# y transposed back through fewer PSUM banks, two expert halves summed in PSUM, nine early products of zeros, and an instruction order drawn from 42 candidates

## The chip, the core and the metric

The kernel runs on one core of one Trainium2 chip. The metric is the device time of one execution in microseconds. Five engines work side by side, each through its own list of instructions in a fixed order: TensorE (PE, with its weight loads shown as PEld), VectorE (DVE), ScalarE (ACT), GpSimd (POOL) and SyncE (SP), which issues the DMAs. They wait for each other by semaphores only.

## What is computed

Attention with a top-32 mask per row, then a mixture of four experts weighted per token, then a gated product with a last projection. All in fp32.

```python
# attention: B, H, S, D = 2, 8, 576, 64
scores = scale * np.matmul(q, k.transpose(0, 1, 3, 2))
kth = np.partition(scores, -top_k, axis=-1)[..., -top_k:-top_k + 1]   # top_k = 32
scores = np.where(scores >= kth, scores, -1e9)
attn = softmax(scores); x = attn @ v
# experts: N, D, E, F = 1152, 512, 4, 1024
for e in range(E):
    out += p[:, e:e + 1] * (np.maximum(x @ w1[e], 0.0) @ w2[e])
# gated: d_ff = 1536
return ((x @ w_a) * (x @ w_b)) @ w_out
```

## The kernel before

The 1152 tokens are nine tiles of 128 (eight regular ones and one that mixes the last 64 rows of both batches). They are cut into four groups of 1, 2, 3 and 3 tiles. Attention runs over groups, head pairs (four) and tiles, 36 steps in all; each step has two heads. For each head PE makes scores of 128 x 576 (`scores`, matmuls of 288 columns), ACT copies them to SBUF (L618), DVE finds the 32 largest by four MAX8 (L638) with three MATCH_REPLACE8 between them (L646), ACT and POOL mask and exponentiate (L669, L673, L677, L688), PE transposes the weights and multiplies by v. The result of one head pair goes to `xf` (group 0) or `xs` (the others) as the input of the experts.

The experts of group 0 (`plain`) run in fp32 straight from the loaded weights. Those of groups 1 to 3 (`experts`) split every operand into a high part (a rounded copy made by ACT, L804) and a low part (a subtraction on POOL or, for the last group, on DVE, L805), and multiply three times. `first` makes one 128-row piece of x @ w1 in a bank of PSUM; ACT and DVE empty it into a high and a low part (L875, L879). `second` multiplies four such pieces (half of F) by w2, 12 matmuls of 512 columns into one bank; DVE then scales the bank by the expert's share and adds it to y in SBUF (L897; the very first time it only scales, L895). So each expert has two halves and each half of each tile one such addition.

When a group's y is complete, `replace` transposes it back to columns: for each of four blocks of 128 columns it takes one PSUM bank, makes one transpose per tile of the group, and ACT (L917) and DVE (L921) empty the bank into the high and low halves of `xs`. The call is deferred (`pending`): it is issued behind the first weight unit of the next group, or in `gated`, ahead of its third block of columns. `gated` is the last stage and runs over all nine tiles. Its own weights are unpacked by ACT and DVE beforehand (`d_unit`).

PSUM has eight banks of 512 fp32 columns. Three of them form the pool `m` (`ms`), from which `first`, `second`, `plain`, `gated` and `replace` all take their banks in the order in which they were asked for; two pairs (`att`) and one bank (`o`) belong to attention.

The order of the instructions is not written by hand: every helper adds an operation with an assumed duration, a key and what it waits for, and `Plan.order` runs through time as a list scheduler, per engine taking the ready operation with the smallest key whose buffers are free. What it gives is the order in which the program is emitted; on the chip each engine then follows its list.

Of the kernel before, what the change touches and what calls it, by code (L numbers as in the profile page):

```python
# [2 lines left out]

# [31 lines left out]
class Slots:  # L35
# [13 lines left out]

    def settle(self):  # L50
        self.queue.sort(key=lambda t: t.need)
        for i, t in enumerate(self.queue):
            t.n = i

# [14 lines left out]
class Op:  # L69
    __slots__ = ("engine", "hold", "lag", "key", "emit", "waits", "after", "tiles", "n", "start", "left", "at", "nbytes", "port", "since")  # L70
# [6 lines left out]

class Plan:
    def __init__(self):
        self.ops = []  # L80

    def add(self, engine, hold, emit, key, after=(), tiles=(), lag=100, nbytes=0, port=False):
        op = Op()
        op.engine, op.hold, op.lag, op.key, op.emit = engine, hold, lag, key, emit
        op.waits = list({id(a): a for a in after if a is not None}.values())
        op.tiles = list({id(t): t for t in tiles}.values())
        op.after, op.n, op.start, op.nbytes, op.port, op.since = [], len(self.ops), None, nbytes, port, 0.0
        for t in op.tiles:
            t.users += 1
        self.ops.append(op)  # L90
        return op

    def order(self):
        for op in self.ops:
            op.left, op.at = len(op.waits), op.since
            for w in op.waits:
                w.after.append(op)
# [69 lines left out]
        while len(done) < len(self.ops):  # L167
            moved = False
            for engine in free:
# [73 lines left out]
LATE = 2  # L243
SLACK = 1200
# [4 lines left out]
def body(tc, q, k, v, probs, w1, w2, wa, wb, wo, out):  # L249
    nc = tc.nc  # L250
# [97 lines left out]
    atts = Slots("att", [ps[:, 3 + 2 * i:5 + 2 * i] for i in range(2)])  # L348
    os_ = Slots("o", [ps[:, 7]])
# [486 lines left out]
    def second(hts, units, t0, after):  # L836

        p = ms.tile()
        last = None
        N = len(hts)  # L840
        for i, ((h, hd, n), (u, ud, uv, part)) in enumerate(zip(hts, units)):
            def emit(i=i, h=h, n=n, uv=uv, part=part):
# [3 lines left out]
                for m, (l, r) in enumerate(((hhi, whi), (hhi, wlo), (hlo, whi))):  # L846
                    mm(p.ap, l, r, start=(i == 0 and m == 0), stop=(i == N - 1 and m == 2))
# [7 lines left out]
    def experts(c):  # L855
# [7 lines left out]
        yd = {}  # L863
        for e in range(E):

            late = 2 if c == len(GROUPS) - 1 else c == len(GROUPS) - 2 and e >= LATE
            for f0 in range(0, F, 512):
# [22 lines left out]
                for t in range(T):  # L890
                    p, o = second(hts, units, t * 128, ())
                    i = TILES.index(tiles[t])
                    yv = lambda t=t: y.ap[:, t * DM:(t + 1) * DM]
                    if e == 0 and f0 == 0:
# [10 lines left out]
    def replace(c, y, yd):  # L905
        T = len(GROUPS[c])
        cs = columns_of(c)
        for a in range(KD):
            p = ms.tile()

            def emit(a=a, p=p):
                for t in range(T):
                    tr(p.ap[:, t * 128:(t + 1) * 128], y.ap[:, t * DM + a * 128:t * DM + (a + 1) * 128], ident)

            o = tensor(T * TURN_F, emit, 1000 + nxt(), list(yd.values()), [p, y])
# [3 lines left out]
            lo = vector(  # L919
                dve(T * 128),  # L920
                lambda a=a, p=p: nc.vector.tensor_tensor(xs[:, 1, a, cs], p.ap[:, 0:T * 128], xs[:, 0, a, cs], op=ALU.subtract),  # L921
                -1000, [hi], [p],
            )
            ydone[c, a] = [hi, lo]
# [195 lines left out]
```

## Time and profile before

| | |
|---|---|
| median of 3 runs | 850.61 us (850.32 to 910.58) |
| the profiled execution | 849.56 us, span 847.8 us |
| PE busy | 817.2 us (96%) |
| DVE busy | 715.7 us (84%) |
| ACT busy | 537.5 us (63%) |
| POOL busy | 267.5 us (32%) |
| moved by DMA | 117.06 MB |

The profile is of one execution. Busy time counts an engine's instructions; a row of the timeline is a run of like instructions with its start, its length, and in brackets how long the engine stood idle before it and for whom it waited. The granted clock of TensorE has two levels here, 1.2 and 2.4 GHz.

### The profile page before, as it was taken

Reading aid. Unit: us, or ns where it says so; the run is one execution under the profiler, and the core shown is the slowest. Engines: PE = TensorE matmul, PEld = TensorE weight load, DVE = VectorE, ACT = ScalarE, POOL = GpSimd, SP = SyncE. Lnnn points to the kernel's source line nnn. Section 1 sums busy time; section 2 is a strip of 40 time slices with the busy share of each in tenths; the row PEclk is TensorE's granted clock in tenths of the full one; section 3 lists DMA queues with packets and bytes.
Section 4 is the critical chain, followed back from the end, with each engine's and each line's share of the span. In section 5 each row is a group of like instructions: output and inputs, shape, how many; then the busy total and the mean of one; then the engine's idle time right before and its main releaser. Section 6 shows DMA issues by size and latency. Waiting matters only on the chain.

```text
span 847.8 us, 14175 instructions
## 1 busy us (share of the span) xinstructions
PE 817.2 (96%) x5168; PEld 728.4 (86%) x5168; DVE 715.7 (84%) x1387; ACT 537.5 (63%) x1034; POOL 267.5 (32%) x250
## 2 busy tenths in 40 slices
PE   6689999999999999999999999999999999999997
PEld 5467787788988888999889898899898989999996
DVE  7999999999999999999969998555435888989823
ACT  6888887998999898788665654334225535344220
POOL 3534343879897966755210000000000000000000
PEclk9999999999999999999999999999999999999999
DMA  5849877755554544333246654343001322323003
GB/s 170 287 115 310 306 241 231 230 174 173 147 191 132 156 169 151 105 101 100 78 131 193 208 177 160 124 131 118 2 1 50 100 68 82 100 83 93 26 1 111
DMA packets 83509, 117.06 MB, mean 138 GB/s; under 512 B 10608, under 2 KB 54640, under 8 KB 83440
## 3 DMA queue, kind: packets, MB, share of 16 engines
q1 hardware_dynamic: 83440, 116.17, 43.8%
q8 instruction: 40, 0.66, 0.3%
q14 instruction: 29, 0.24, 0.1%
HBM read 109.07 MB, written 7.08 MB: 137 GB/s over the span
## 4 chain that ended last, share of the span: by engine, by line
PE 78%; DVE 10%; ACT 7%; issue 2%; POOL 1%; DMA 0%; POOLq 0%; ACTq 0%; DVEq 0%
PE ps L373 72%; PE ps L376 6%; DVE low L638 3%; DVE low L646 2%; DVE mid L805 1%; ACT low L688 1%; ACT low L618 1%; ACT low L669 1%; ACT big L429 1%; ACT low L677 1%; ACT big L570 1%; DVE mid L879 1%; ACT low L743 1%; POOL big L433 1%; POOL low L673 1%
## 5 line engine op out<-in xcount | busy, mean ns | idle before, releaser
L373 PE MATMUL ps<-xs,mid 128*128 128x384 f32 (+1 forms) x1152 | 204.1, 322 | 1.3 <-DVE mid L879 1.3
L638 DVE MAX8 low<-low 128x8 f32<-128x576 f32 x288 | 203.6, 747 | 2.1 <-ACT low L618 2.0
L373 PE MATMUL ps<-mid 128*128 128x512 f32 x768 | 198.3, 395 | 0.3 <-POOL mid L805 0.3
L373 PEld LDWEIGHTS ps<-xs,mid 128*128 128x128 f32 x1152 | 186.0, 191 | 9.6 <-DVE mid L879 1.5
L373 PEld LDWEIGHTS ps<-mid 128*128 128x128 f32 x768 | 139.5, 188 | 24.0 <-DVE mid L879 0.7
L646 DVE MATCH_REPLACE8 low<-low 128x576 f32<-128x576 f32 x216 | 159.3, 744 | 0.0
L373 PE MATMUL ps<-xs,big 128*128 128x384 f32 x864 | 152.6, 335 | 0.0
L373 PEld LDWEIGHTS ps<-xs,big 128*128 128x128 f32 x864 | 150.2, 188 | 1.2 <-DVE xs L921 0.2
L804 ACT ACTIVATE mid<-raw 128x1024 fp32r<-128x1024 f32 x96 | 101.5, 1061 | 43.4 <-issue 27.2
L805 POOL TENSOR_TENSOR mid<-raw,mid 128x1024 fp32r<-128x1024 f32 x48 | 115.3, 2407 | 15.3 <-ACT mid L804 11.3
L673 POOL TENSOR_TENSOR low<-low 128x576 f32<-128x576 f32 x70 | 99.3, 1437 | 27.9 <-ACT low L669 27.8
L875 ACT ACTIVATE mid<-ps 128x384 fp32r<-128x384 f32 (+1 forms) x96 | 43.6, 455 | 51.4 <-PE ps L373 46.0
L373 PE MATMUL ps<-big,mid 128*128 128x512 f32 x324 | 76.0, 391 | 0.0
L373 PEld LDWEIGHTS ps<-big,mid 128*128 128x128 f32 x324 | 60.5, 188 | 12.5 <-DVE low L1053 0.4
L879 DVE SCALAR_TENSOR_TENSOR mid<-ps,mid 128x384 fp32r<-128x384 f32 (+1 forms) x96 | 48.4, 507 | 26.0 <-ACT mid L875 25.5
L805 DVE TENSOR_TENSOR mid<-raw,mid 128x1024 fp32r<-128x1024 f32 x48 | 58.5, 1220 | 9.6 <-ACT mid L804 8.8
L688 ACT ACTIVATE low<-low 128x576 f32<-128x576 f32 x70 | 51.4, 778 | 12.4 <-DVE low L685 12.4
L618 ACT ACTIVATE low<-ps 128x576 f32<-128x576 f32 x72 | 46.8, 650 | 18.4 <-POOL low L673 13.1
L669 ACT ACTIVATE low<-low 128x576 f32<-128x576 f32 x70 | 51.9, 778 | 9.8 <-POOL low L663 9.7
L897 DVE SCALAR_TENSOR_TENSOR ys<-ps,pr,ys 128x512 f32<-128x512 f32 x56 | 41.8, 746 | 18.9 <-PE ps L373 18.3
L1050 ACT ACTIVATE low<-ps 128x384 f32<-128x384 f32 x36 | 17.7, 491 | 62.8 <-PE ps L373 62.7
L376 PE MATMUL ps<-identr,low 128*128 128x128 f32 (+1 forms) x360 | 50.0, 279 | 5.2 <-ACT low L688 4.6
(87 smaller groups left out, 1050.9 us busy)
## 6 DMA issues: line engine op xcount, KB each, us to landing
raw<-in_moe_w_dram SPq DMA_DIRECT2D x122, 512.0 KB, 3.8
big<-kscr SPq DMA_DIRECT2D x20, 576.0 KB, 4.8
low<-in_v_dram SPq DMA_DIRECT2D x24, 256.0 KB, 3.8
low<-in_moe_w_a_dram SPq DMA_DIRECT2D x12, 512.0 KB, 4.3
low<-in_moe_w_b_dram SPq DMA_DIRECT2D x12, 512.0 KB, 3.8
low<-in_moe_w_out_dram SPq DMA_DIRECT2D x12, 512.0 KB, 3.6
kscr<-big SPq DMA_DIRECT2D x8, 576.0 KB, 4.9
ys<-in_moe_w_dram SPq DMA_DIRECT2D x6, 512.0 KB, 4.8
```

Source lines behind the costliest of these rows:

```text
L373: nc.tensor.matmul(out, l, r, **kw)
L376: nc.tensor.transpose(out, a, i)
L618: S, lambda: nc.scalar.activation(s.ap.rearrange("p (c n) -> p c n", c=2), at.ap[:, :, 0:HALF], AF.Copy),
L638: 62 + 1.04 * width, lambda at=at, cs=cs: nc.vector.max(m8v()[:, x, cs], at()), key + 0.02 * r, [done],
L646: lambda at=at, cs=cs: nc.vector.match_replace(out=src[1](), in_to_replace=m8v()[:, x, cs], in_values=at(), imm_value=LOW),
L669: S, lambda x=x, s=s: nc.scalar.activation(e[x].ap, s.ap, AF.Relu, bias=endv()[:, x, 1:2], scale=-STEEP),
L673: pool_(S), lambda x=x, s=s: nc.gpsimd.tensor_tensor(e[x].ap, s.ap, e[x].ap, op=ALU.subtract), ks, [a], [s, e[x]]
L688: S, lambda x=x: nc.scalar.activation(e[x].ap, e[x].ap, AF.Copy, scale=sums.ap[:, x:x + 1]),
L804: hi = scalar(1024, lambda: nc.scalar.activation(u.ap[:, 0:1024], r.ap, AF.Copy), 500 + s, [ld], [u, r], sbuf=True)
L805: sub = lambda eng: eng.tensor_tensor(u.ap[:, 1024:2048], r.ap, u.ap[:, 0:1024], op=ALU.subtract)
L875: n, lambda h=h, p=p: nc.scalar.activation(h.ap[:, 0:n], p.ap[:, 0:n], AF.Relu), -1000, [o], [h, p]
L879: lambda h=h, p=p: nc.vector.scalar_tensor_tensor(h.ap[:, n:2 * n], p.ap[:, 0:n], 0.0, h.ap[:, 0:n], op0=ALU.max, op1=ALU.subtract),
```

## The change

Four things change.

- `replace` packs G blocks of columns into one bank: 4 for group 0 (one tile), 2 for group 1 (two tiles), 1 for the groups of three tiles. ACT and DVE empty a bank with one instruction each. For groups 2 and 3 the banks come from a new pool `mls`, the five banks that attention used; that pool may hand out a bank only when attention's pools are done.
- For the last group, `second` keeps the sum of an expert's two halves in one bank of `mls`: the first half starts the accumulation, the second ends it, and only then DVE scales and adds (24 additions become 12).
- Before anything else PE makes nine products of 128 x 256 out of a block of zeros, which DVE writes first (`blank`).
- `Plan.best` builds 42 orders. In each, every operation is assumed to end late by a random amount of up to 25 (in the planner's ns), from a certain stage of time on; each order is replayed three times with random lateness of engines and DMAs, and the one with the smallest mean replayed end is emitted.

```diff
+ORDERS, RERUNS, SHAKE, LATE_ENGINE, LATE_DMA, LOG = 42, 3, 25.0, 40.0, 800.0, False
+    def best(self):
+        found = None
+        for r in range(ORDERS):
+            draw = random.Random(r)
+            since = STAGES[r * len(STAGES) // ORDERS]
+            for op in self.ops:
+                if r:
+                    op.late = found[3][op.n] if found[4][op.n] < since else draw.uniform(0.0, SHAKE)
+            got = self.order()
+            mean = sum(self.rerun(got, random.Random(i)) for i in range(RERUNS)) / RERUNS
+            if found is None or mean < found[0]:
+                found = mean, got, {id(t): t.slot for op in got for t in op.tiles}, [op.late for op in self.ops], [op.start for op in self.ops]
...
-                    end = now + op.hold + op.lag
+                    end = now + op.hold + op.lag + op.late
...
-    atts = Slots("att", [ps[:, 3 + 2 * i:5 + 2 * i] for i in range(2)])
-    os_ = Slots("o", [ps[:, 7]])
+    atts = Slots("att", [ps[:, 3 + 2 * i:5 + 2 * i] for i in range(2)], "psum", [(3, 5), (5, 7)])
+    os_ = Slots("o", [ps[:, 7]], "psum", [(7, 8)])
+    mls = Slots("ml", [ps[:, 3 + i] for i in range(5)], "psum", [(3 + i, 4 + i) for i in range(5)])
+    atts.rank, os_.rank, mls.rank = 0, 0, 1
...
-    def second(hts, units, t0, after):
-        p = ms.tile()
-        last = None
+    def second(hts, units, t0, after, bank=None, begin=True, end=True, last=None):
+        p = bank or ms.tile()
...
-                    mm(p.ap, l, r, start=(i == 0 and m == 0), stop=(i == N - 1 and m == 2))
+                    mm(p.ap, l, r, start=(begin and i == 0 and m == 0), stop=(end and i == N - 1 and m == 2))
...
-                    p, o = second(hts, units, t * 128, ())
+                    if c == len(GROUPS) - 1:
+                        if f0 == 0:
+                            sums_[t] = mls.tile(), None
+                        end = f0 + 512 == F
+                        sums_[t] = second(hts, units, t * 128, (), sums_[t][0], f0 == 0, end, sums_[t][1])
+                        if not end:
+                            continue
+                        p, o = sums_[t]
+                    else:
+                        p, o = second(hts, units, t * 128, ())
...
-        for a in range(KD):
-            p = ms.tile()
+        G = max(1, 4 // T) if T != 3 else 1
+        for a0 in range(0, KD, G):
+            p = mls.tile() if c >= len(GROUPS) - 2 else ms.tile()
...
-                T * 128, lambda a=a, p=p: nc.scalar.activation(xs[:, 0, a, cs], p.ap[:, 0:T * 128], AF.Copy), -1000, [o], [p]
+                w, lambda a0=a0, pv=pv: nc.scalar.activation(xs[:, 0, a0:a0 + G, cs], pv(), AF.Copy), -1000, [o], [p]
...
+    zeros_ = xs[:, 0, 0, 0:384]
+    blank = vector(300, lambda: nc.vector.memset(zeros_.bitcast(F32), 0.0), -1e6, (), ())
+    idle = ms.tile()
...
+    for i in range(FILL):
+        late = i >= 9
+        op = tensor(
+            120 if late else 215, lambda: mm(idle.ap[:, 0:256], zeros_[:, 0:128], zeros_[:, 128:384], start=True, stop=True),
+            1e9 + i, [blank], [idle],
+        )
+        op.since = 46e3 if late else 2.4e3
...
-    for op in plan.order():
+    for op in plan.best():
         op.emit()
```

How the instructions stand now is shown at four places. The first is the start of PE's list, after the change; `xs` holds the zeros, `identr` the identity of a transpose, `big` the split q and k. Before, the list begins with the second of these rows.

```order
L457 MATMUL ps<-xs 128x256 x9
L460 MATMUL ps<-identr,big 128x128 x4
L460 MATMUL ps<-identr,big 128x64
L460 MATMUL ps<-identr,big 128x128 x6
L460 MATMUL ps<-identr,big 128x64
L460 MATMUL ps<-identr,big 128x128 x2
L457 MATMUL ps<-big 128x288 x8
```

Nine products have come in front; the transposes of k and q and the first scores follow as before.

The second is PE at the place where group 0's y is transposed back (`identr,ys`), among the first matmuls of group 1's experts (`xs,mid`), before:

```order
L373 MATMUL ps<-low,vrem_72 64x128 x2
L373 MATMUL ps<-big 128x288 x4
L373 MATMUL ps<-xs,mid 128x256 x3
L376 MATMUL ps<-identr,ys 128x128 x2
L373 MATMUL ps<-xs,mid 128x256 x6
L376 MATMUL ps<-identr,ys 128x128 x2
L373 MATMUL ps<-xs,mid 128x256 x24
```

and the same place after the change:

```order
L457 MATMUL ps<-xs,mid 128x256 x6
L460 MATMUL ps<-identr,ys 128x128 x4
L457 MATMUL ps<-big 128x288 x4
L457 MATMUL ps<-low 64x128 x8
L457 MATMUL ps<-low,vrem_72 64x128 x2
L457 MATMUL ps<-big 128x288 x4
L457 MATMUL ps<-xs,mid 128x256 x30
L457 MATMUL ps<-mid 128x512 x12
```

The four transposes have moved together, ahead of a step of attention.

The third is PE where group 3's y is transposed back, among the first matmuls of `gated` (`xs,big`), before:

```order
L373 MATMUL ps<-mid 128x512 x3
L373 MATMUL ps<-xs,big 128x384 x42
L376 MATMUL ps<-identr,ys 128x128 x3
L373 MATMUL ps<-xs,big 128x384 x3
L376 MATMUL ps<-identr,ys 128x128 x9
L373 MATMUL ps<-xs,big 128x384 x93
```

and after:

```order
L457 MATMUL ps<-mid 128x512 x30
L457 MATMUL ps<-xs,big 128x384 x48
L460 MATMUL ps<-identr,ys 128x128 x12
L457 MATMUL ps<-xs,big 128x384 x96
L457 MATMUL ps<-big,mid 128x512 x51
```

All twelve transposes stand together, six matmuls further on.

The fourth is SP's list of loads in group 0's expert stage (`raw` is a weight load of 512 KB, `low` q or v, `big` a split k that comes back from HBM), before:

```order
L355 DMA big<-kscr 128x1152
L355 DMA raw<-in_moe_w_dram 128x2x512 x2
L355 DMA raw<-in_moe_w_dram 128x4x256 x2
L355 DMA low<-in_q_dram 128x2x64
L355 DMA low<-in_q_dram 128x2x128
L355 DMA low<-in_v_dram 128x2x256
```

and after:

```order
L439 DMA big<-kscr 128x1152
L439 DMA raw<-in_moe_w_dram 128x2x512 x2
L439 DMA low<-in_q_dram 128x2x64
L439 DMA low<-in_q_dram 128x2x128
L439 DMA raw<-in_moe_w_dram 128x4x256 x2
L439 DMA low<-in_v_dram 128x2x256
```

Two loads of weights have moved behind two loads of q.

## Rows read from the trace of the kernel before

**Rows 1.** The page: span, busy time (share) xinstructions, chain by engine.
```profile
span 847.8 us, 14175 instructions
...
PE 817.2 (96%) x5168; PEld 728.4 (86%) x5168; DVE 715.7 (84%) x1387; ACT 537.5 (63%) x1034; POOL 267.5 (32%) x250
...
PE 78%; DVE 10%; ACT 7%; issue 2%; POOL 1%; DMA 0%; POOLq 0%; ACTq 0%; DVEq 0%
```
**Rows 2.** Busy time by stretch: us, busy (xinstructions), PE clock, DMA share, GB/s.
```profile
core 0: us, PE busy (x) PEld busy (x) DVE busy (x) ACT busy (x) POOL busy (x), PEclk, DMA share, GB/s
4.40:60.00 55.60, 40.59 (x279) 33.92 (x280) 52.84 (x121) 43.19 (x97) 21.59 (x29) 1.00 0.63 194
60.00:150.00 90.00, 87.96 (x655) 68.23 (x654) 89.49 (x194) 74.56 (x155) 39.31 (x47) 1.00 0.82 267
150.00:300.00 150.00, 148.04 (x1125) 131.36 (x1126) 147.52 (x322) 138.71 (x278) 129.92 (x97) 0.99 0.57 176
300.00:480.00 180.00, 178.87 (x1230) 160.90 (x1229) 171.79 (x332) 137.26 (x264) 73.66 (x64) 1.00 0.42 131
480.00:490.00 10.00, 8.97 (x52) 8.08 (x51) 9.97 (x18) 7.85 (x14) 0.00 (x0) 1.00 0.55 185
490.00:620.00 130.00, 130.00 (x656) 117.64 (x655) 82.52 (x115) 48.21 (x68) 0.00 (x0) 1.00 0.36 114
620.00:630.00 10.00, 9.61 (x58) 8.99 (x58) 4.00 (x8) 3.86 (x8) 0.00 (x0) 1.00 0.01 2
630.00:840.00 210.00, 210.00 (x1113) 197.03 (x1112) 153.62 (x282) 81.76 (x151) 0.00 (x0) 1.00 0.22 67
```
**Rows 3.** Timeline: start, length, engine, operation; output transfers at the end.
```profile
835.77 9.35 SPq L355 DMA_DIRECT2D out_dram<-low  x8
```
**Rows 4.** Waits of PE between 60 and 830 us: total us, times, longest.
```profile
PE ps L376 <- DVE mid L879: 2.1, 3, 1.0
PE ps L373 <- DVE mid L879: 1.3, 1, 1.3
...
PE ps L376 <- DVE xs L921: 0.2, 1, 0.2
```
**Rows 5.** Timeline of PE, transposes of group 0's y.
```profile
161.23 0.52 PE L376 MATMUL ps<-identr,ys 128*128 128x128 f32 x2 [0.17 <-DVE xs L921]
163.07 0.39 PE L373 MATMUL ps<-xs,mid 128*128 128x256 f32 x1 [1.32 <-DVE mid L879]
```
**Rows 6.** Timeline of PE, transposes of the y of groups 1, 2 and 3.
```profile
308.58 0.44 PE L376 MATMUL ps<-identr,ys 128*128 128x128 f32 x2 [0.97 <-DVE mid L879]
...
487.03 0.55 PE L376 MATMUL ps<-identr,ys 128*128 128x128 f32 x3 [0.98 <-DVE mid L879]
...
626.23 1.01 PE L376 MATMUL ps<-identr,ys 128*128 128x128 f32 x6 [0.39 <-DVE low L1053]
```
**Rows 7.** By line: DVE's additions to y, count, busy us, mean ns.
```profile
L897 DVE SCALAR_TENSOR_TENSOR ys<-ps,pr,ys 128x512 f32<-128x512 f32 x56 | 41.8, 746 | 18.9 <-PE ps L373 18.3
```
**Rows 8.** Timeline of the first 10 us, and of score matmuls at 37.88 us.
```profile
1.33 1.01 DVE L397 CAST identr<-xf 128x128 fp32r<-128x128 f32 x1 [1.33 <-POOL xf masks.py:199]
...
4.49 2.59 PE L376 MATMUL ps<-identr,big 128*128 128x128 f32 x14 [4.49 <-DVE big L431]
...
6.00 0.55 DVE L431 TENSOR_TENSOR big<-low,big 64x384 fp32r<-64x384 f32 x1 [0.42 <-ACT big L429]
6.48 0.41 DVE L566 CAST big<-ps 128x256 fp32r<-128x256 f32 x1
...
7.03 2.26 PE L373 MATMUL ps<-big 128*128 128x288 f32 x8
...
9.05 0.76 DVE L638 MAX8 low<-low 128x8 f32<-128x576 f32 x1 [1.50 <-ACT low L618]
...
37.88 0.80 PE L373 MATMUL ps<-big 128*128 128x288 f32 x4
```
**Rows 9.** Waits of PE's weight loads between 60 and 830 us.
```profile
PEld ps L376 <- ACT low L688: 4.0, 13, 0.6
...
PEld ps L373 <- ACT low L677: 0.2, 1, 0.2
```

More of the change, by code (lines that the diff above doesn't have):

```diff
@@ L48, in tile, with again @@
         return t
+    def again(self):
+        self.free, self.next = set(range(len(self.aps))), 0
+        for t in self.queue:
+            t.slot, t.users = None, 0
     def settle(self):
@@ L53, in settle, with cells @@
             t.n = i
+    def cells(self, i):
+        if self.spans is None:
+            return [(self.name, i)]
+        a, b = self.spans[i]
+        return [(o.name, j) for o in self.beside for j, (c, d) in enumerate(o.spans) if c < b and a < d]
     @property
@@ L69 @@
 class Op:
-    __slots__ = ("engine", "hold", "lag", "key", "emit", "waits", "after", "tiles", "n", "start", "left", "at", "nbytes", "port", "since")
+    __slots__ = ("engine", "hold", "lag", "key", "emit", "waits", "after", "tiles", "n", "start", "left", "at", "nbytes", "port", "since", "late")
 SEEN, SEEN_PE = 45, 130
 ISSUE, LAND, GBS, LANES = 500, 2100, 320.0, 8
+STAGES = 0.0, 50e3, 110e3, 170e3, 230e3, 300e3, 400e3
+ORDERS, RERUNS, SHAKE, LATE_ENGINE, LATE_DMA, LOG = 42, 3, 25.0, 40.0, 800.0, False
 class Plan:
     def __init__(self):
-        self.ops = []
+        self.ops, self.freed = [], {}
     def add(self, engine, hold, emit, key, after=(), tiles=(), lag=100, nbytes=0, port=False):
@@ new lines, in rerun @@
+    def rerun(self, got, draw):
+        free, end, dma, users = {}, {}, 0.0, {}
+        last = 0.0
+        for op in got:
+            t = free.get(op.engine, 0.0)
+            for w in op.waits:
+                t = max(t, end[id(w)] + (SEEN_PE if op.engine == "PE" else SEEN))
+            for b in op.tiles:
+                u = users.get(id(b))
+                if u is None:
+                    u = users[id(b)] = [max([self.freed.get(k, 0.0) for k in b.slots.cells(b.slot)] or [0.0])]
+                t = max(t, u[0] + (SEEN_PE if op.engine == "PE" else SEEN))
+            if op.engine == "SP":
+                free["SP"] = t + ISSUE
+                dma = max(dma, t + ISSUE) + op.nbytes / GBS
+                e = dma + LAND + draw.uniform(0.0, LATE_DMA)
+            else:
+                free[op.engine] = t + op.hold
+                e = t + op.hold + op.lag + (draw.uniform(0.0, LATE_ENGINE) if op.engine != "PE" else 0.0)
+            end[id(op)] = e
+            last = max(last, e)
+            for b in op.tiles:
+                k = (b.slots.name, b.slot)
+                self.freed[k] = max(self.freed.get(k, 0.0), e)
+        self.freed.clear()
+        return last
@@ L94, in order @@
+    def order(self):
+        every = {id(t.slots): t.slots for op in self.ops for t in op.tiles}.values()
+        for s in every:
+            s.again()
+            s.beside = [o for o in every if s.region is not None and o.region == s.region]
+        for op in self.ops:
+            op.after, op.start = [], None
+            for t in op.tiles:
+                t.users += 1
         for op in self.ops:
@@ L243 @@
 LATE = 2
+FILL = 9
 SLACK = 1200
@@ L890, in experts @@
                 for t in range(T):
-                    p, o = second(hts, units, t * 128, ())
+                    if c == len(GROUPS) - 1:
[6 more added lines that the diff above has]
+                        p, o = sums_[t]
+                    else:
+                        p, o = second(hts, units, t * 128, ())
                     i = TILES.index(tiles[t])
                     yv = lambda t=t: y.ap[:, t * DM:(t + 1) * DM]
-                    if e == 0 and f0 == 0:
+                    if t not in yd:
                         emit = lambda yv=yv, p=p, i=i, e=e: nc.vector.tensor_scalar(yv(), p.ap, pr[:, i, e:e + 1], None, op0=ALU.mult)
```

33 lines of the change are left out of this document (23 added, 10 removed).

## The prediction

> **What bounds the kernel now.** I read the page first: its span, the busy shares and the chain that ended last [rows 1]. TensorE (PE) is busy for 817.2 of 847.8 us and carries 78% of the chain; VectorE (DVE) is busy for 715.7 us. So time is gained only where PE stands still, or where its work shrinks. The change leaves PE's matmuls as they are (it adds nine small ones), so the question is where the 847.8 - 817.2 = 30.6 us of idle PE lie.
>
> The busy times by stretch answer it [rows 2]. PE does nothing for 4.4 us and then 40.59 of 55.60 us: 19.4 us are lost by 60 us. There DVE is the fuller engine with 52.84 us, most of it the top-32 search of the first attention tiles, without which no expert matmul can begin. From 60 us on PE is full: it misses 2.0 us of 90, 2.0 of 150, 1.1 of 180, 1.0 of 10 and 0.4 of 10, and nothing in 490 to 620 and 630 to 840 us. The last 4.8 us of its idle time are the output's way home: the last eight output transfers are issued over 9.35 us from 835.77 us on [rows 3], and the change leaves them alone.
>
> PE's own waits between 60 and 830 us say what these 6.4 us were for (eight rows, the first, the second and the last stand in [rows 4]): 2.1 + 1.3 us for DVE's L879, 0.2 us for L921, and with the 0.39 us for L1053 [rows 6] that makes 4.0 us; the other 2.4 us went to ScalarE (ACT), by far the most, and POOL. The 4.0 us all lie at one kind of place: the four points at which the result y of a token group is transposed back (replace). The timeline shows the worst of each: behind the second pair of transposes for group 0 PE waits 1.32 us, with 0.17 us ahead of them [rows 5]; for group 1 it waits 0.97 us, for group 2 0.98 us and for group 3 0.39 us [rows 6]. The 2.1 us of L879 leave 2.1 - 0.97 - 0.98 = 0.17 us for a shorter stop of group 1. Together that is 4.0 us. The cause is visible in the code: replace takes four banks of the pool `m`, which has three, so the next bank is there only when ACT (L917 or L875) and then DVE (L921 or L879) have emptied one.
>
> **The change, part by part.** The sum is made against the profiled execution's own 849.56 us (span 847.8 us and 1.8 us around it); the median of the runs shown is 850.61 us, 1.05 us above it.
>
> *y back through few banks.* Group 0 now puts its four transposes into one bank, group 1 its eight into two; in the rows of the order the four of group 0 stand in one block, with attention matmuls and thirty expert matmuls behind them. Two of three banks stay free for those, so 0.17 + 1.32 and 0.17 + 0.97 us fall away. Groups 2 and 3 take as many banks as before, but out of five others that attention has left by then; 0.98 us fall away. For group 3 twelve transposes stand in one row, and the first matmul behind them needs the first piece emptied by ACT and then by DVE, so I keep 0.3 of its 0.39 us. Sum: -4.0 + 0.3 = -3.7 us. An idle row starts only when the last matmul has drained: the row of two transposes lasts 0.52 us [rows 5], two issues take about 0.2, so each of the stops hides up to 0.3 us more. Bounds: nothing (rival one) and -3.7 - 5 x 0.3 = -5.2 us. I take -4.2 us, near the upper end, since the stalls are on PE itself. The wider evacuations (one of 512 columns in place of four of 128) save ACT and DVE some time; neither is waited for there, so that is costed at nothing. What hides it is PE's queue of expert matmuls; without that cover a 512-column evacuation would hold up the first reader of xs, which for groups 0 and 1 is hundreds of us away.
>
> *The last group's expert halves added in PSUM.* Twelve of the 56 additions at L897, 0.746 us each [rows 7], go away: 9.0 us of DVE. They lie between 490 and 620 us, where PE is busy for 130.00 of 130 us and DVE for 82.52 [rows 2]. PE is not waiting for them, so 9 us of DVE are worth close to nothing: bounds 0 and the few tenths that the banks of `m` gain, since second matmuls no longer use them. I take -0.2 us.
>
> *Early products of zeros.* Nine matmuls of 256 columns and one memset on DVE. The score matmuls of 288 columns stand 8 in 2.26 us at 7.03 us, and 4 in 0.80 us from 37.88 us on [rows 8]: taking off the drain of one, that is 240 ns against about 133 ns, so PE starts at the level of 1.2 GHz and is at that of 2.4 GHz by 38 us. The nine cost 9 x 213 = 1.9 us at the low clock. DVE's first instruction ends at 2.34 us; the memset takes between nothing and 0.41 x 384/256 = 0.6 us by the cast of 256 columns [rows 8]; so the products end between 4.3 and 4.9 us, up to 0.4 us behind the first transpose's start at 4.49 us. That is covered: the scores at 7.03 us wait for DVE's cast at 6.48 us, which stands behind DVE's split of a k piece that ACT has ready late (6.00 us, after 0.42 us of waiting for ACT), not for PE. If the clock has risen by 7 us, the first four score matmuls, for which ACT's copy of the scores waits, end 4 x 0.107 + 0.1 = 0.5 us earlier, and the first top-32 search at 9.05 us with them; since DVE then stays full to 60 us, all of it moves. Bounds: +0.4 us (cover gone, clock not risen) and -0.6 us; I take -0.5 us.
>
> The Trainium skill, "TensorE: Matmul & The Clock Gate", section "Part 4: PE-mode transpose", speaks against this part: PE transposes do not count as activity for the clock as matmuls do, and between the products of zeros and the scores stand fourteen transposes. By it the gain is 0 and the sum below half a microsecond smaller. The trace agrees as far as it goes: fourteen transposes and eight matmuls from 4.49 us on left the clock low [rows 8].
>
> *The order.* Of all waits of PE's weight loads between 60 and 830 us, leaving out those for "issue" and for the lines of the y places (L879, L921, L1053), thirteen rows from 4.0 to 0.2 us remain, 12.4 us together (the first and the last in [rows 9]). That is the most another order could win beyond the y places (a load's wait partly overlaps a running matmul). The printed order keeps the pattern: the start is row for row the same behind the nine products, and attention's pieces come in the same succession, with expert matmuls shifted between them. Bounds: -12.4 us, and on the bad side rival three's 12 us. I take a fifth of the gain, -2.5 us.
>
> Sum: -4.2 - 0.2 - 0.5 - 2.5 = -7.4 us; 849.56 - 7.4 = 842.2, taken as 842 us.
>
> **Rivals.** *One: the time is given back.* What PE gains at 161 and 307 us it must spend on expert matmuls whose weights are split by ACT and POOL. POOL is busy for 129.92 of 150 us there, ACT for 138.71, DVE for 147.52 [rows 2]. If that chain sets the pace, PE waits 1 to 2 us later instead. Then only group 2 and 3 keep theirs (-1.1 us), with the clock's -0.5: 848 us. Against it: PE is busy for 148.04 of the same 150 us with its two stops there in it, so weights are at hand when it can use them.
>
> *Two: the order wins more.* Were 11 of the 12.4 us gone, the sum would be -4.9 - 11 = -15.9, or 834 us; with half of them (6.2), 838 us. For it: those waits are many and short, which is what a search over orders can shift. Against: the two orders are much alike.
>
> *Three: the other side.* The order moves weight loads on SP behind others: in the piece shown two loads of `raw` that stood ahead of two q loads now stand behind them. A load of 512 KB takes 2.0 us at the 267 GB/s of 60 to 150 us, where the DMA engines are 82% busy [rows 2], and group 0's plain experts read `raw` directly. A load that comes late with no cover costs 2.0 us; from four of them on (8 us) the gain is gone, and ten would be 862 us. Against: none of the eight rows of PE's waits names a DMA [rows 4], and only a few loads trade places. I put it at six late loads, 12 - 7.4 = 4.6 us slower: 854 us.
>
> **How the numbers follow.** The forecast (838 to 846 us) 0.55; given back (846 to 851) 0.20; the order wins more (831 to 838) 0.14; slower (851 and up) 0.11. The range 835 to 852 us leaves out about 0.08 below and 0.10 above. Faster by over 2% means below 833.6 us: 0.05, the far end of rival two. Slower by over 2% means above 867.6 us: 0.03, rival three with more than twelve late loads. Within 2%, about what a measurement of this kernel can tell from no change, 0.92.
>
> **What would show it.** Right: no PE wait above 0.4 us behind a `ps<-identr,ys` row; PE idle in 60 to 830 us near 3 us in place of 6.4; L897 44 times; the first MAX8 near 8.5 us, and scores before 9 us at 133 ns each. Wrong: those scores still at 240 ns (the clock's term is 0); new PE waits for L805, L804 or a DMA in 150 to 480 us (rival one or three); or a span under 836 us with the waits for L688 and L618 gone (rival two).

## The result, and the profile after

| | before | after |
|---|---|---|
| median of its runs, us | 850.47 (847.58 to 910.58) | 841.40 (841.12 to 841.84) |
| profiled execution, us (span) | 849.56 (847.8) | 841.12 (839.3) |

The ratio after to before is 0.9911, with an interval of [0.9899, 0.9924]: 6.5 to 8.6 us less, and 8.4 us between the two profiled executions; that is within 2%. (One disturbed run of before, at 910.58 us, does not enter the ratio.) The forecast was 842 us. As the experiments show, two of its four terms had the wrong size and a third came out right only by the luck of one draw.

In the code after the change the lines have new numbers: L373 became L457, L376 L460, L618 L702, L638 L722, L688 L772, L805 L889, L879 L962, L897 L990, L921 L1020, L963 L1063 and L1053 L1153.

The page of after (span; busy time, share and instructions; the chain that ended last), beside [rows 1]:

```profile
span 839.3 us, 14126 instructions
...
PE 817.1 (97%) x5177; PEld 729.6 (87%) x5177; DVE 707.0 (84%) x1371; ACT 536.5 (64%) x1029; POOL 266.0 (32%) x250
...
PE 80%; DVE 16%; ACT 3%; issue 1%; POOL 0%; DVEq 0%; POOLq 0%; ACTq 0%
```

PE's busy time has stayed (817.2 and 817.1 us), so the whole gain of 8.5 us is idle time: 30.6 us have become 839.3 - 817.1 = 22.2. DVE's share of the chain has grown from 10% to 16%; that will matter below.

Busy time by stretch of after (the columns are those of [rows 2]):

```profile
4.40:60.00 55.60, 41.95 (x284) 34.83 (x282) 53.55 (x123) 44.14 (x98) 21.87 (x30) 0.97 0.64 198
60.00:150.00 90.00, 88.95 (x665) 69.70 (x666) 90.00 (x194) 76.22 (x156) 41.24 (x47) 1.00 0.85 273
150.00:300.00 150.00, 149.49 (x1135) 132.30 (x1133) 149.35 (x323) 138.81 (x278) 133.24 (x100) 1.00 0.57 182
300.00:480.00 180.00, 180.00 (x1242) 162.45 (x1241) 170.76 (x322) 136.04 (x262) 66.54 (x62) 1.00 0.40 124
480.00:490.00 10.00, 10.00 (x51) 8.98 (x50) 9.90 (x18) 5.51 (x11) 0.00 (x0) 1.00 0.56 184
490.00:620.00 130.00, 129.99 (x667) 118.74 (x666) 75.45 (x109) 51.36 (x76) 0.00 (x0) 1.00 0.37 111
620.00:630.00 10.00, 10.00 (x60) 10.00 (x59) 2.77 (x6) 2.04 (x4) 0.00 (x0) 1.00 0.00 0
```

PE misses 1.0 us of 90 (2.0 before), 0.5 of 150 (2.0), nothing of 180 (1.1), nothing of the two short stretches (1.0 and 0.4), and 13.65 us between 4.4 and 60 us (15.0). DVE has no free time from 60 to 150 us. The rows give the idle time as follows: 1.4 us less between 4.4 and 60 us, 5.0 us less from there to 630 us, and 2.0 us less ahead of 4.4 us, where the nine products now stand. Those nine add 2.1 us to PE's busy time (2.40 to 4.49 us), and yet its total has not grown: 2.1 us also went out of what the trace counts as busy.

PE's waits between 60 and 830 us in after, all of them, beside [rows 4] (line waited for, total us, times, longest):

```profile
PE ps L457 <- ACT low L1063: 0.5, 1, 0.5
PE ps L460 <- ACT low L772: 0.4, 1, 0.4
PE ps L457 <- POOL mid L889: 0.4, 1, 0.4
PE ps L460 <- ACT low L702: 0.2, 1, 0.2
```

All rows of the y places (DVE's L962 and L1020, the former L879 and L921, and L1153) are gone, 4.0 us; the rest has shrunk from 2.4 to 1.5 us. The timeline of PE at the four places, beside [rows 5, 6] (start, length, operation, count; a wait would stand in brackets):

```profile
155.92 0.60 PE L460 MATMUL ps<-identr,ys 128*128 128x128 f32 x4
...
299.61 0.60 PE L460 MATMUL ps<-identr,ys 128*128 128x128 f32 x4
...
478.92 1.14 PE L460 MATMUL ps<-identr,ys 128*128 128x128 f32 x9
...
617.07 1.47 PE L460 MATMUL ps<-identr,ys 128*128 128x128 f32 x12
```

No row has a wait. Nine transposes take 1.14 us here; before, six of the same group took 1.08 us:

```profile
484.97 1.08 PE L376 MATMUL ps<-identr,ys 128*128 128x128 f32 x6
487.03 0.55 PE L376 MATMUL ps<-identr,ys 128*128 128x128 f32 x3 [0.98 <-DVE mid L879]
```

A short stop inside a row of matmuls, and the drain of the last matmul ahead of a stop, count as busy, so part of the 2.1 us went here. The larger part, 1.3 us, is the clock. In before, PE ran nothing but two transposes from 161.06 to 163.07 us, at group 0's stops, and at 163.7 us the granted clock fell to the level of 1.2 GHz for 3.4 us; it is the 0.99 of the row for 150 to 300 us in [rows 2]. The matmuls behind the stop, and busy time by stretch with the clock (0.51), in before:

```profile
163.07 4.63 PE L373 MATMUL ps<-xs,mid 128*128 128x256 f32 x24 [1.32 <-DVE mid L879]
...
163.70:167.20 3.50, 3.50 (x19) 3.50 (x19) 3.22 (x7) 2.48 (x3) 2.71 (x4) 0.51 0.62 189
```

As many of the same matmuls at the same place in the run with the new `replace` alone (below):

```profile
160.56 3.33 PE L457 MATMUL ps<-xs,mid 128*128 128x256 f32 x24
```

That is 1.3 us less: in before, fifteen of them stand 213 ns apart in place of 118 to 120. In the three profiled executions that keep the old `replace` (before, and the sums and the search alone) the clock falls at this place, at 163.7 to 164.5 us; in the eleven with the new one it does not fall anywhere between 60 and 830 us. Which stops bring it about is not shown: with the longer subtractions (below) PE stops for 0.59 and 1.42 us without it.

To size a stop wholly I laid the two traces over each other by work done: each matmul counts with its undisturbed step to the next, and the time at which the same amount of work is done is compared. By this working after gains 2.6 us at 160 to 165 us (group 0's y), 1.5 at 300 to 310 (group 1), 1.6 at 485 to 490 (group 2) and 0.6 at 620 to 630 (group 3), 6.3 us in all where the wait rows say 4.0; some 1.5 us by 160 us, 0.4 between 310 and 480, 0.3 at 490 to 500, 0.02 from there to 620 us, nothing net between 165 and 300 us (about 1 us lost to 250 and won again). At group 0's place the excess over the wait rows is 2.6 - 1.5 = 1.1 us, no more than the clock cost there. At the three others it is 3.7 - 2.5 = 1.2 us for four stops, 0.3 us each, in drains and short stops.

The start of after, DVE and PE (before: [rows 8]):

```profile
1.97 0.38 DVE L1179 MEMSET xs<- 128x384 f32 x1
...
2.40 2.29 PE L457 MATMUL ps<-xs 128*128 128x256 f32 x9 [2.40 <-DVE xs L1179]
...
4.49 2.60 PE L460 MATMUL ps<-identr,big 128*128 128x128 f32 x14
...
6.88 2.25 PE L457 MATMUL ps<-big 128*128 128x288 f32 x8
...
8.90 0.76 DVE L722 MAX8 low<-low 128x8 f32<-128x576 f32 x1 [1.44 <-ACT low L702]
```

PE works without a gap from 2.40 us on, and the eight scores still take 2.25 us, 240 ns each as before. In this execution the clock has not risen by then.

### The profile page after: what moved, and what is told of

The parts are those of the page before. It is cut to its first block, busy times and chain, and to the rows that moved or that the text cites. A ratio compares the mean times of both kernels' runs of the same rounds, so it can differ in the third digit from the quotient of the medians.

```text
span 839.3 us, 14126 instructions
## 1 busy us (share of the span) xinstructions
PE 817.1 (97%) x5177; PEld 729.6 (87%) x5177; DVE 707.0 (84%) x1371; ACT 536.5 (64%) x1029; POOL 266.0 (32%) x250
## 4 chain that ended last, share of the span: by engine, by line
PE 80%; DVE 16%; ACT 3%; issue 1%; POOL 0%; DVEq 0%; POOLq 0%; ACTq 0%
PE ps L457 75%; DVE low L722 8%; DVE low L730 7%; PE ps L460 4%; ACT low L772 1%; ACT mid L888 0%; POOL mid L889 0%; ACT low L827 0%; ACT low L702 0%; ACT low L753 0%; DVE low L793 0%; ACT low L761 0%; DVE low L1171 0%; DVE ys L1079 0%; DVE xs L867 0%
## 5 line engine op out<-in xcount | busy, mean ns | idle before, releaser
L722 DVE MAX8 low<-low 128x8 f32<-128x576 f32 x288 | 203.9, 747 | 1.7 <-ACT low L702 1.7
L457 PE MATMUL ps<-xs,mid 128*128 128x384 f32 (+1 forms) x1152 | 203.9, 321 | 0.0
L457 PE MATMUL ps<-mid 128*128 128x512 f32 x768 | 197.5, 395 | 0.4 <-POOL mid L889 0.4
L457 PEld LDWEIGHTS ps<-xs,mid 128*128 128x128 f32 x1152 | 185.1, 189 | 9.2 <-issue 1.9
L457 PEld LDWEIGHTS ps<-mid 128*128 128x128 f32 x768 | 139.6, 188 | 23.7 <-POOL mid L889 1.0
L457 PE MATMUL ps<-xs,big 128*128 128x384 f32 x864 | 152.6, 335 | 0.0
L457 PEld LDWEIGHTS ps<-xs,big 128*128 128x128 f32 x864 | 150.2, 188 | 1.5 <-DVE xs L1020 0.3
L889 POOL TENSOR_TENSOR mid<-raw,mid 128x1024 fp32r<-128x1024 f32 x48 | 115.3, 2408 | 12.9 <-ACT mid L888 8.8
L889 DVE TENSOR_TENSOR mid<-raw,mid 128x1024 fp32r<-128x1024 f32 x48 | 59.4, 1237 | 23.5 <-ACT mid L888 23.0
L457 PE MATMUL ps<-big,mid 128*128 128x512 f32 x324 | 76.1, 391 | 0.0
L457 PEld LDWEIGHTS ps<-big,mid 128*128 128x128 f32 x324 | 60.5, 188 | 12.6 <-DVE low L1171 0.6
L962 DVE SCALAR_TENSOR_TENSOR mid<-ps,mid 128x384 fp32r<-128x384 f32 (+1 forms) x96 | 48.0, 506 | 23.0 <-ACT mid L958 22.8
L772 ACT ACTIVATE low<-low 128x576 f32<-128x576 f32 x70 | 51.1, 773 | 13.1 <-DVE low L769 13.1
L753 ACT ACTIVATE low<-low 128x576 f32<-128x576 f32 x70 | 52.2, 776 | 6.7 <-POOL low L747 6.7
L761 ACT ACTIVATE low<-low 128x576 f32<-128x576 f32 x70 | 54.3, 778 | 2.1 <-POOL low L757 1.8
L460 PE MATMUL ps<-identr,low 128*128 128x128 f32 (+1 forms) x360 | 51.1, 284 | 4.4 <-ACT low L772 3.8
L702 ACT ACTIVATE low<-ps 128x576 f32<-128x576 f32 x72 | 46.4, 649 | 11.9 <-POOL low L757 6.6
```

The source lines that it names most:

```text
L457: nc.tensor.matmul(out, l, r, **kw)
L460: nc.tensor.transpose(out, a, i)
L702: S, lambda: nc.scalar.activation(s.ap.rearrange("p (c n) -> p c n", c=2), at.ap[:, :, 0:HALF], AF.Copy),
L722: 62 + 1.04 * width, lambda at=at, cs=cs: nc.vector.max(m8v()[:, x, cs], at()), key + 0.02 * r, [done],
L753: S, lambda x=x, s=s: nc.scalar.activation(e[x].ap, s.ap, AF.Relu, bias=endv()[:, x, 1:2], scale=-STEEP),
L761: lambda x=x: nc.scalar.activation(e[x].ap, e[x].ap, AF.Exp, bias=endv()[:, x, 0:1], scale=scale, accum_out=sums.ap[:, x:x + 1]),
```

## The experiments

The kernel before stood at 849.2 to 849.4 us beside them; ratios are to it. Edits are shown against the kernel after the change. Where an edit must leave the order of the rest alone, it is made where the instruction is issued, behind the planner.

### Without the products

```diff
-            120 if late else 215, lambda: mm(idle.ap[:, 0:256], zeros_[:, 0:128], ...),
+            120 if late else 215, lambda: None,
```

The memset is left out too; the order of all else is the same.

> The changed kernel with the same order of instructions, but the nine products of zeros and the memset of zeros left out (nothing of the result hangs on them). My theory after the result: the clock never rose in time (the first scores still stand 240 ns apart in the changed kernel), so the products are worth nothing: within 0.5 us of the changed kernel, ratio to the kernel before 0.991, first MAX8 within 0.1 us of 8.90 us. Rival (my prediction's term): they are worth 0.5 us or more through something else in the first 60 us: 0.5 to 1 us slower than the changed kernel, first MAX8 at about 9.05 us.

841.87 us (841.26 to 842.44), 0.9919 [0.9897, 0.9941]. The first MAX8 starts at 8.99 us, against 8.90 with the products and 9.05 before, and the scores again take 2.25 us for eight. So the products are worth no more than the spread of the runs.

### One part at a time

Without the search, all else kept:

```diff
-    for op in plan.best():
+    for op in plan.order():
```

> The changed kernel with one order drawn without random lateness in place of the best of 42. Theory: most of the 8.5 us gained comes from y going back without stops (about 6 us by the comparison of the traces), the search gives about 2: so 843 to 844 us, ratio 0.993 to 0.994. Rival: the search carries the gain: 846 us or more, ratio above 0.996.

845.86 us (845.14 to 846.88), 0.9966 [0.9955, 0.9978]. The search is worth 4.5 us in the changed kernel.

The new `replace` alone; the three other parts are switched off, so that it is the kernel before with this one part:

```diff
-FILL = 9
+FILL = 0
...
-                    if c == len(GROUPS) - 1:
+                    if False:
...
-    blank = vector(300, ...)
-    idle = ms.tile()
...
-    for op in plan.best():
+    for op in plan.order():
```

> The kernel before with y's way back alone changed (few banks for groups 0 and 1, attention's five banks for groups 2 and 3), no search, no products, additions of the last group in SBUF as before. Theory: 5 to 6 us faster than before, 844.5 to 845.5 us, ratio 0.994, and no PE wait over 0.4 us next to the transposes of y. Rival (time given back): the stops go, but PE waits for POOL, ACT or DVE instead, 848 us or more, ratio above 0.997.

845.80 us (845.44 to 846.35), 0.9960 [0.9946, 0.9973]: 3.5 us, the same as without the search, so that sums and products add nothing to it beyond the spread. By work done the four places win 2.6 + 1.8 + 1.6 + 0.6 = 6.6 us, but the trace loses 1.9 us between 165 and 305 us, nearly all of it at 200 to 250, and 0.9 between 310 and 480; at 160 us it stands 0.25 us behind before. (The 2 us that it loses at 40 to 50 us go with the clock, which is low in it from 42.5 to 49.3 us and not in before; it had won most of that elsewhere by 160 us.) One of the losses in PE's timeline:

```profile
237.78 1.43 PE L460 MATMUL ps<-identr,low 128*128 128x128 f32 x10 [0.46 <-ACT low L772]
...
239.64 0.73 PE L457 MATMUL ps<-mid 128*128 128x512 f32 x2 [0.20 <-POOL mid L889]
```

PE comes earlier and then waits for ACT's softmax copies and POOL's split of weights. This is rival one, in part.

The sums in PSUM alone. The search, `FILL` and the memset are switched off in the same way, the sums stay, and `replace` is the old one:

```diff
-        G = max(1, 4 // T) if T != 3 else 1
+        G = 1
...
-            p = mls.tile() if c >= len(GROUPS) - 2 else ms.tile()
+            p = ms.tile()
```

> The kernel before with the last group's expert halves added in PSUM alone, in banks that attention has left. Theory: DVE is not what PE waits for there, so the twelve additions saved (9 us of DVE) are worth nothing: 850 us, ratio 0.999 to 1.001. Rival: freer banks of the pool of three give PE 1 us or more: ratio 0.998 or less.

847.59 us (845.83 to 848.68), 0.9983 [0.9973, 0.9994]: 1.7 us, where the theory had next to nothing and the rival 1 us or more. By work done it is all at 485 to 500 us (1.7 us) and 620 to 630 (0.2), and 0.05 us in between, where DVE has its 9 us less. Busy time by stretch:

```profile
480.00:490.00 10.00, 10.00 (x58) 8.97 (x57) 9.97 (x18) 7.60 (x14) 0.00 (x0) 1.00 0.48 169
490.00:620.00 130.00, 130.00 (x661) 118.55 (x660) 73.86 (x103) 48.74 (x69) 0.00 (x0) 1.00 0.35 113
```

PE has no idle time left at 480 to 490 us, although `replace` is the old one. The last group's `second` no longer takes banks of `m`, so the y of group 2, which is transposed back among those matmuls, finds one. It is the same stop that the new `replace` takes away, and it can be won only once.

The search alone: `plan.best()` stays, and the old `replace`, the old `second` and `FILL = 0` are set with the lines shown above.

> The kernel before with the best of 42 orders alone; y's way back, the additions in SBUF and the start as before. In the changed kernel the search was worth 4.4 us (without it 845.9 us against 841.4). Theory: it is worth as much by itself, for it removes short waits that lie all over the attention stretch: 845 to 846 us, ratio 0.995. Rival: much of its worth is that it takes back what PE lost at 200 to 310 us after the stops of y had gone (1.9 + 0.9 us in the runs without search), so by itself it gives 2 us or less: 847.5 us or more, ratio 0.998 or above.

847.44 us (846.48 to 849.10), 0.9981 [0.9969, 0.9992]: 2 us, what the rival said. But the list of operations is another here, so the same seeds give other delays: this is a draw of its own, and not the order of the change without the other parts. Its wait rows show what it could not shift:

```profile
PE ps L460 <- DVE mid L962: 3.6, 4, 1.6
PE ps L457 <- DMA ys<-in_moe_w_dram: 0.7, 1, 0.7
```

The stops for banks stay in this order too (3.6 us behind L962), and a load comes 0.7 us late.

### How much of the order is a choice, how much a draw

The worst of the same 42 orders in place of the best:

```diff
-            if found is None or mean < found[0]:
+            if found is None or mean > found[0]:
```

> The changed kernel, but of the orders the one with the largest mean replayed end is emitted (each stage of draws starts from it). Theory: the replay ranks orders as the chip does, at least roughly, so this one is slower than the order without lateness (845.9 us): 848 us or more. Rival: the ranking says little about the chip, any drawn order is about as good: 842 to 846 us.

853.07 us (851.43 to 853.60), 1.0037 [1.0023, 1.0051]: 11.7 us behind the best, and behind the kernel before. Its waits of PE between 150 and 300 us, all of them:

```profile
PE ps L457 <- POOL mid L889: 4.5, 3, 2.5
PE ps L457 <- ACT low L827: 0.3, 1, 0.3
```

In after the same view has one row, 0.4 us for L889. So the replay tells a bad order from a good one, and the largest single part of what makes this one bad is POOL's split of weights coming late: PE is busy for 145.07 of these 150 us, against 149.49 in after, which is 4.4 of the 10.6 us between the two profiled executions.

The start of this trace matters as well, PE and then DVE:

```profile
2.40 2.29 PE L457 MATMUL ps<-xs 128*128 128x256 f32 x9 [2.40 <-DVE xs L1179]
4.49 2.21 PE L460 MATMUL ps<-identr,big 128*128 128x128 f32 x14
6.88 1.44 PE L457 MATMUL ps<-big 128*128 128x288 f32 x8 [0.18 <-DVE big L650]
...
8.37 0.76 DVE L722 MAX8 low<-low 128x8 f32<-128x576 f32 x1 [0.97 <-ACT low L702]
```

The same nine products and fourteen transposes start at the same times as in after, but here the clock rises at 5.9 us: the eight scores take 1.44 us and the first MAX8 starts at 8.37 us, as the prediction had it. It is the only one of the seven profiled executions with nine products in which this happens; in the five without products the scores are at 240 ns. By 9.3 us the clock is low again.

The best of 42 others:

```diff
-            draw = random.Random(r)
+            draw = random.Random(1000 + r)
```

> The changed kernel with other random draws (seeds 1000 to 1041 in place of 0 to 41), best of 42 again. Theory: the search finds an order of like worth: 840 to 843 us. Rival: the order of the changed kernel is a lucky draw: 844 us or more.

846.49 us (846.13 to 847.22), 0.9967 [0.9955, 0.9979]: no better than without a search. Against this one other set of draws, the order of the change is a lucky draw, by some 5 us. The planner saw most of that itself: with `LOG` set it prints each order's mean replayed end, and the best is 839.6 us for the change, 843.2 us here, and 845.5 us for the unsearched order. On the chip the 2.3 us between the last two are not there.

The best of 126, drawn more widely:

```diff
-ORDERS, RERUNS, SHAKE, LATE_ENGINE, LATE_DMA, LOG = 42, 3, 25.0, 40.0, 800.0, False
+ORDERS, RERUNS, SHAKE, LATE_ENGINE, LATE_DMA, LOG = 126, 3, 150.0, 40.0, 800.0, False
...
-            draw = random.Random(r)
+            draw = random.Random(21000 + r)
```

> The changed kernel with 126 orders instead of 42, random lateness of up to 150 instead of 25, and other draws. The replay by which the orders are ranked puts its best order ahead of the changed kernel's. Theory: the ranking holds on the chip as it did for the worst order (853.1 us) and the other draws (846.5 us): 836 to 839.5 us, ratio 0.984 to 0.988. Rival: below the best of 42 the differences that the replay sees are smaller than its errors: 840.5 us or more.

840.87 us (840.27 to 841.58), 0.9903 [0.9887, 0.9918]. The replay had put this order 4 us ahead of the one of the change (835.5 against 839.6 us); the chip makes them equal, so for this pair the ranking shows nothing more. So a second search of the changed kernel came out at 841 us too; it had three times as many orders and a wider lateness, so it does not say how often 42 draws would.

### What stands on the path at group 0's y

24 matmuls more on PE, ahead of the four transposes and in the same bank; the order of the rest is the same:

```diff
+                if T == 1:
+                    for _ in range(24):
+                        mm(p.ap[:, 0:128], identr, identr, start=True, stop=True)
```

> The changed kernel with the same order, and 24 products of the identity by itself put into the bank of group 0's y ahead of its transposes at 156 us: some 2 to 2.6 us more for PE there (24 x 85 to 110 ns), nothing of the result hangs on them. Theory (PE's work alone sets the end from 60 us on): the end moves by what they last, 843.4 to 844 us, ratio 0.9935 to 0.9945. Rival (the stretch has slack, since DVE is full there too): 842 us or less.

843.84 us (843.64 to 844.20), 0.9933 [0.9916, 0.9950]. The timeline of PE:

```profile
156.08 2.79 PE L457 MATMUL ps<-identr 128*128 128x128 f32 x24
158.71 0.62 PE L460 MATMUL ps<-identr,ys 128*128 128x128 f32 x4
```

158.71 - 156.08 = 2.63 us of PE cost 2.4 us at the median: there is no slack on PE here, and what is won at this y place can be kept.

DVE's subtraction of the same piece made five times in place of once:

```diff
-                lambda a0=a0, pv=pv: nc.vector.tensor_tensor(xs[:, 1, a0:a0 + G, cs], pv(), ..., op=ALU.subtract),
+                lambda a0=a0, pv=pv: [nc.vector.tensor_tensor(xs[:, 1, a0:a0 + G, cs], pv(), ..., op=ALU.subtract)
+                    for _ in range(5 if T == 1 else 1)],
```

> The changed kernel with the same order; DVE's one subtraction that empties group 0's y (0.68 us at 157.4 us) is made five times over, so DVE has 4 x 0.6 = 2.4 us more to do at the very place where 2.6 us more of PE cost 2.4 us. Theory: PE's work alone sets the end there, DVE has the rest of the attention stretch to catch up: within 0.7 us of the changed kernel, 841 to 842.2 us. Rival: DVE, busy for 149 of 150 us there, is as much a bound as PE: 843 us or more.

844.48 us (843.59 to 845.20), 0.9941 [0.9924, 0.9959]: 3.1 us more than after, where I had DVE's work hidden behind PE's queue. DVE, then PE:

```profile
158.70 3.57 DVE L1021 TENSOR_TENSOR xs<-ps,xs 128x512 fp32r<-128x512 f32 x5
```

```profile
162.33 2.41 PE L457 MATMUL ps<-xs,mid 128*128 128x256 f32 x18 [0.59 <-DVE xs L1021]
166.16 3.38 PE L457 MATMUL ps<-mid 128*128 128x512 f32 x12 [1.42 <-DVE mid L962]
```

The first wait is for the bank that the subtractions hold. The second is for L962: DVE runs its list in order, L962 and the searches stand behind the subtractions, and it must finish before `second` has its input. By work done PE loses 2.5 us at 160 to 165 us. The profiled execution, at 845.20 us, lies 4.1 us behind that of after, and 1.9 us of this are lost by 46 us, ahead of the edit: its clock rises first at 38.1 us (34.8 in after) and is low again from 41.5 to 48.3 us (41.6 to 45.0). So 2.5 of the 3.1 us are the edit's at this place; the rest is the size of such differences at the start.

### An earlier clock

Eighteen products in place of nine, and the memset as DVE's first instruction; the order of the rest is that of after:

```diff
-            120 if late else 215, lambda: mm(...),
+            120 if late else 215, lambda: [mm(...) for _ in range(2)],
...
-    for op in plan.best():
+    order = plan.best()
+    nc.vector.memset(zeros_.bitcast(F32), 0.0)
+    for op in order:
```

> The changed kernel with the same order; the memset of zeros stands first on DVE and there are eighteen products instead of nine, so that PE works without a gap from about 1.1 us to the end of the first scores. Theory: the nine products came too late or too few to raise the clock before the first scores; with eighteen it rises, the scores at 6.9 us stand about 133 ns apart and the first MAX8 comes 0.4 to 0.6 us earlier, at 8.3 to 8.5 us; the time falls by as much, 841 us. Rival: the fourteen transposes between the products and the scores leave the clock low, scores 240 ns apart, nothing gained.

841.16 us (840.94 to 841.58), 0.9906 [0.9891, 0.9921]. The start of PE, and the first search on DVE:

```profile
1.31 4.21 PE L457 MATMUL ps<-xs 128*128 128x256 f32 x18 [1.31 <-DVE xs L1204]
5.32 2.19 PE L460 MATMUL ps<-identr,big 128*128 128x128 f32 x14
...
7.35 1.57 PE L457 MATMUL ps<-big 128*128 128x288 f32 x8
...
8.83 0.76 DVE L722 MAX8 low<-low 128x8 f32<-128x576 f32 x1 [0.82 <-ACT low L702]
```

Now the clock does rise: eight scores in 1.57 us against 2.25. But the products hold the first transposes back from 4.49 to 5.32 us, and the first MAX8 gains 0.07 us, short of the 0.4 to 0.6 us of the theory. Nor does the level last: the granted clock falls at 10.1 us, and the next twelve transposes take 2.35 us, as they do in after.

```profile
11.58 2.35 PE L460 MATMUL ps<-identr,big 128*128 128x128 f32 x12 [2.66 <-POOL big L517]
```

Both together (eighteen products early, best of 126):

> The order with more draws and the eighteen early products together. Theory: if the clock rises before the first scores, 0.4 to 0.6 us less than with more draws alone, the first MAX8 at 8.3 to 8.5 us. Rival: the same as with more draws alone within 0.3 us.

840.28 us (839.74 to 840.90), 0.9895 [0.9881, 0.9910], the fastest kernel run. The start of its scores and the first search:

```profile
6.99 1.43 PE L457 MATMUL ps<-big 128*128 128x288 f32 x8
...
8.47 0.76 DVE L722 MAX8 low<-low 128x8 f32<-128x576 f32 x1 [0.96 <-ACT low L702]
```

The run to hold it against is the one with more draws alone: its first MAX8 starts at 8.88 us, so 0.4 us are won there, and the median is 0.6 us lower, both as the theory said. But the runs of the two overlap (839.74 to 840.90, 840.27 to 841.58), so the gain in time is a hint and not shown.

## Why the prediction came out right, and where it did not

The forecast of 842 us for 841.12 of the profiled run is near, but its terms were not: 4.2 + 0.2 + 0.5 + 2.5 stand against about 6.3, 0, 0 and 2.

- **y back: mechanism right, size too small.** All stops for banks went, as said, and no PE wait over 0.4 us stands behind a `ps<-identr,ys` row. The term was 4.2 us with an upper bound of 5.2; by work done the places gave 6.3 us in after and 6.6 alone. Two steps failed. The larger one is a term that the sum does not have: the clock fell behind group 0's stop, and as many matmuls took 4.63 us there in before and 3.33 without the stop. The prediction sized that stop by its wait rows and the drain alone. The drains themselves were sized well: it allowed up to 0.3 us per stop, and the four stops of the other groups hid 0.3 us each; but it took only 0.5 us of its 1.5. The smaller one: I kept 0.3 us for group 3 on the ground that the first matmul behind its transposes needs the first piece; PE has no such wait in the trace: ACT starts to empty the first piece at 617.60 us, while the twelve transposes still run, and only a weight load waits, 0.27 us for L1020, beside running matmuls.
- **Wider evacuations "costed at nothing": right here, for a wrong reason.** I named PE's queue as the cover. The run with four more subtractions shows that it does not cover DVE at this place: 3.57 - 0.68 = 2.9 us more of DVE cost PE 2.5 us there, and the kernel 3.1 at the median. The one subtraction of 512 columns takes 0.68 us in after, the four of 128 before took 2 x 0.48 us, so up to 0.3 us of the gain at this place may be DVE's; no run separates it.
- **Sums in PSUM: 9 us of DVE worth nothing, as said.** Both with and without the new `replace`, 490 to 620 us did not move. Alone the part gives 1.7 us by freeing banks of `m`, more than the "few tenths" of my bound, but at the stop that the other part takes away as well. In the sum the term is 0.
- **Products of zeros: 0.5 us taken, 0 in the profiled execution.** The step that failed is the condition "If the clock has risen by 7 us": in after it had not. The rule of the Trainium skill ("TensorE: Matmul & The Clock Gate", section "Part 4: PE-mode transpose"), that PE transposes don't count for the clock as matmuls do, had given 0, and the trace of after agrees with that outcome: nine products and fourteen transposes left the scores at 240 ns. In the worst of the 42 orders the same nine and fourteen were followed by scores at 133 ns, and with eighteen products they were both times; so the link from the clock to the first search was right, and whether nine products are enough differs between executions. Whether the transposes count is not shown. No pair of runs shows a gain in time beyond the spread.
- **The order: 2.5 us for about 2, not by insight.** My fifth of the waits had no ground in the code. What an order is worth here was measured: 4.5 us over the unsearched order, nothing with one other set of draws, -7.2 us for the worst of the 42. The 2 us are what the comparison by work done leaves beside the y places. The printed order "keeps the pattern", and yet the orders lie 12 us apart.
- **Rival one (time is given back) was partly true** and hidden by the draw: in the unsearched order 6.6 us won at the y places left 3.5. With the change's order nothing net was lost between 165 and 300 us. **Rival two** was true in kind (PE's other waits fell from 2.4 to 1.5 us), not in size. **Rival three** did not occur in after; without the search there is one wait of 0.4 us for a DMA, and with the search in the kernel before one of 0.7 us.
- **The marks.** L990 (the former L897) stands 44 times, as forecast. PE's idle time from 60 to 830 us is 1.6 us, not 3. The first MAX8 is at 8.90 us, not 8.5.

What stays open: how often a search of 42 finds an order as good as this one, and why some do. The views show that the poor ones wait for POOL's L889, ACT's copies and DVE's L962, not what in the draw brings that about. The first 60 us also vary with the times at which the clock rises and falls: in the profiled executions the longer subtractions are 1.9 us behind after by 46 us, with the same order up to there. This blurs differences of that size.

## What to carry to other kernels

Where an engine is full and stops only for a bank, count the stop as more than its wait row: drains and short stops hide in busy time, and the clock may fall behind it, which shows in the granted clock of a narrow stretch; here 4.0 us of rows were 6.3 us. Two parts that free the same resource at the same place were worth the larger one here, not the sum, so try each alone and both together. And an order found by search is a draw: compare it with the search under other draws before its gain is put down to the method, and judge other edits with the order held fixed.

## What the runs showed of the hardware

- With eighteen products without a gap from 1.31 us on, the clock had risen by the scores (7.35 and 6.99 us) in both profiled executions; with nine from 2.40 us, in one of seven; without products, in none of five. The transposes in between are the same fourteen. At the higher level eight scores take 1.43 to 1.57 us, at the lower 2.25, and in all three it is low again by 12 us.
- A stop can cost time behind it too: in before, PE waited 0.17 and 1.32 us at group 0's y with two transposes in between, then the granted clock was low for 3.4 us and 24 matmuls took 4.63 us in place of 3.33. The clock fell there in all three executions with the old `replace`.
- A matmul row's busy time isn't pure work: six transposes with a short stop in them took 1.08 us, nine without took 1.14.
- DVE can be on the path beside PE where attention's searches and the experts overlap: in after it is busy for 90.00 us of 90 from 60 to 150 us and 149.35 of the next 150, and at 158.7 us 2.9 us more of it cost PE 2.5 us, while 2.6 us more of PE cost 2.4.
